# Attention followed by a gated MLP on one core: batch 0 in two K halves, weight blocks loaded in turn, a four-sum product form, a searched order

## The chip, the cores and the metric

The kernel runs on one core of one Trainium2 chip. The metric is the device time of one execution in microseconds (us), as a median of several executions. A profiled execution also gives a span, which is some 1.7 us shorter than the timed figure (259.1 against 260.84 us in the profiled run of the kernel before). For a program on one core a run is called slow when it lies over 1.5% above the fastest of its kernel; only fast runs enter the ratios below.

The program keeps its operands in SBUF and puts the products of TensorE in banks of PSUM (the pools with `space=PSUM`), from where VectorE and ScalarE read them. Engine names in the profile are PE (TensorE, the matrix products), PEld (its weight loads, which overlap: 193.8 us beside 241.7 us of PE in a span of 259.1 us in the kernel before), DVE (VectorE), ACT (ScalarE), POOL (GpSimd) and SP or SPq (SyncE, whose queue issues the DMAs).

## The reference

Eight batches, eight heads, 576 positions of 64 numbers each; 32 packed queries `p` per head. Attention packs the keys and values into 32 positions and lets `q` attend to those; a gated MLP follows.

```python
p_packed = sm_attn(p, k, v)                 # 8 x 8 x 32 x 64
out = sm_attn(q, p_packed, p_packed)        # 8 x 8 x 576 x 64, softmax(scale * q kT) v
x = out.transpose(0, 2, 1, 3).reshape(4608, 512)
h = x @ w_in                                # 512 -> 2048
g = h * (1.0 / (1.0 + np.exp(-beta * h)))
return g @ w_out                            # 2048 -> 512, float32
```

## The kernel before

The kernel never forms the attention output. It multiplies the packed values into `w_in` (products `w_ps`, scaled by beta into `W_bf`) and the softmax weights `A2T` into that (`h_ps`, the hidden layer). ScalarE turns `h_ps` into `g_main`. The second layer works on *units* of 256 positions: two for each batch, and two more (`g_rem`) that collect the 64 remaining positions of four batches each.

The instructions are not written in their order. Every piece of work is a task with an engine, an estimated duration, dependences and a rank, and a list scheduler, which runs when the kernel is built, emits them: each engine takes the ready task with the lowest rank. When TensorE has nothing ready before 48 us, it emits a small filler product (`warm_ps`), meant to keep its clock up: the granted clock of the profiled run is 1.00 from 0 to 210 us.

```python
WARM_UNTIL = 48.0
FIRST = "p k0 w_in0 k0r beta w_in2 v0 v0r q0 k1 k1r q0r v1 q1 v1r q1r w_out1 w_in1 w_in3 w_out2 w_out0 w_out3".split()
...
                if not can:
                    if e == "PE" and now < WARM_UNTIL:
                        self.filler()
                        free[e] = now + 0.11
                        moved = True
                    continue
                start(min(can, key=lambda t: t.rank))
```

`FIRST` ranks the first loads. The two units of batch 0 are *plain*: 16 products of 512 columns per half unit are summed in one PSUM bank over all of K, so they need all of `w_out`.

```python
            def product(i, x=x):                       # plan_plain
                ...
                for f in (2 * i, 2 * i + 1):
                    self.mm(st[*unit, "o", x][:], st[*unit, "g"][:, 2 * (f // 8) + x, f % 8, :], self.w_out_bf[:, f, :],
                            start=(f == 0), stop=(f == FT - 1))
            ...
            for i in range(8):
                last = self.task(("p", unit, x, i), "PE", 0.44, ...,
                    made + [("w_out", 2 * i), ("w_out", 2 * i + 1), last], ...)
```

The other 16 units are in *product form*: seven block products in place of eight (Strassen's kind), with sums of operands made on VectorE (`g_sums`, `w_mix`), products in four PSUM banks C, D, A, B, and five takes of 512 columns, four of them on VectorE, that combine the banks in SBUF (`o_sb`).

```python
            if i == 0:                                  # sums of a unit
                nc.vector.tensor_tensor(st[*unit, "S"][:, 0:2], g[:, 0:2], g[:, 2:4], ALU.add)
            elif i == 1:
                nc.vector.tensor_tensor(st[*unit, "S"][:, 2], g[:, 0], g[:, 3], ALU.add)
            else:
                nc.vector.tensor_tensor(g[:, 1:3], g[:, 1:3], g[:, 0:4:3], ALU.subtract)
```

The sums of the first softmax (`z1`) are ten products per batch against a matrix of ones, and their reciprocal is multiplied into the packed values. The last unit of all is a rest unit, stored by four DMAs.

The softmax here doesn't subtract the row's maximum and nothing guards it: scores larger than these inputs give would overflow.

## Time and profile before

| | before |
|---|---|
| time, median (lowest to highest) | 261.65 us (259.98 to 265.47), 3 runs |
| profiled span | 259.1 us |
| filler products of TensorE | 256, all before 50 us |
| VectorE / ScalarE busy | 199.2 us (77%) / 176.1 us (68%) |
| last product ends, span ends | 253.1 us, 259.1 us |

To read it: the busy share of TensorE (93%) counts filler as work. The useful split is between the start, where data is missing, and the rest, where TensorE is hardly ever idle.

### The profile page before, as it was taken

What the parts mean: (1) busy time and instruction counts of PE and PEld (TensorE: products, weight loads), DVE (VectorE), ACT (ScalarE), POOL (GpSimd) and SP (SyncE); (2) the same over time, 40 slices, a digit from 0 to 9 for tenths busy, and PEclk for the clock granted to TensorE, in tenths of its full rate; (3) what the DMA queues carried; (4) which work ended last, traced back from release to release, by engine and by line L of the source; (5) the groups of instructions that cost most, each with busy time, mean ns of one, the idle gap of its engine ahead of it and who ended that gap; (6) DMA issues with size and microseconds to landing.
All of it is one profiled execution on the core that took longest, in us unless ns stands there. A gap on an engine that the chain in (4) does not pass through costs nothing.

```text
span 259.1 us, 6793 instructions
## 1 busy us (share of the span) xinstructions
PE 241.7 (93%) x2897; PEld 193.8 (75%) x2897; DVE 199.2 (77%) x288; ACT 176.1 (68%) x308; POOL 63.4 (24%) x58
## 2 busy tenths in 40 slices
PE   4899689899989999998999999999999999999990
PEld 4897576566554878886778877877889778889880
DVE  6476766887985987796888968979996688665771
ACT  1153579867877878879786987886898768765000
POOL 4320433151440741342315231600900000000000
PEclk9999999999999999999999999999999999999999
DMA  7999999997998998996998999989660102201113
GB/s 225 352 320 268 280 325 384 348 330 183 288 199 237 292 246 235 212 333 148 265 251 263 143 318 291 205 227 272 174 172 7 79 0 83 82 27 60 81 81 81
DMA packets 73471, 54.18 MB, mean 209 GB/s; under 512 B 42065, under 2 KB 66657, under 8 KB 73441
## 3 DMA queue, kind: packets, MB, share of 16 engines
q1 hardware_dynamic: 73440, 53.76, 75.2%
q8 instruction: 22, 0.36, 0.6%
q14 instruction: 9, 0.07, 0.1%
HBM read 37.23 MB, written 9.44 MB: 180 GB/s over the span
## 4 chain that ended last, share of the span: by engine, by line
PE 56%; DMA 20%; SPq 10%; ACT 4%; issue 3%; POOL 3%; DVE 2%; POOLq 0%
PE o_ps L194 31%; PE h_ps L194 14%; DMA k<-in_k_dram 9%; SPq L336 5%; DMA v<-in_v_dram 4%; PE w_ps L194 3%; DMA qT<-q_bf 3%; SPq L250 2%; PE hr_ps L194 2%; DMA q32r<-in_q_dram 2%; DMA v32r<-in_v_dram 2%; PE z_ps L194 2%; PE s_ps L194 1%; SPq L242 1%; ACT g_main L639 1%
## 5 line engine op out<-in xcount | busy, mean ns | idle before, releaser
L639 ACT ACTIVATE g_main<-h_ps 128x512 bf16<-128x512 f32 x128 | 71.1, 596 | 29.5 <-PE h_ps L194 28.6
L194 PE MATMUL h_ps<-A2T,W_bf 128*128 128x256 bf16 x512 | 70.2, 273 | 0.6 <-ACT g_main L639 0.6
L194 PEld LDWEIGHTS <-W_bf 128*128 128x128 bf16 x768 | 57.1, 98 | 12.7 <-issue 4.7
L194 PE MATMUL o_ps<-w_mix,g_main 128*128 128x256 bf16 x448 | 59.5, 273 | 0.0
L194 PEld LDWEIGHTS <-g_main 128*128 128x128 bf16 x512 | 48.2, 98 | 12.5 <-issue 2.9
L600 DVE TENSOR_TENSOR W_bf<-w_ps,beta_bc 128x512 bf16<-128x512 f32 x64 | 41.5, 682 | 5.7 <-PE w_ps L194 5.2
L194 PEld LDWEIGHTS <-g_sums 128*128 128x128 bf16 x384 | 36.4, 98 | 5.5 <-issue 1.4
L209 ACT ACT_TABLE_LOAD x28 | 35.9, 1283 | 1.2 <-PEq L1067 0.7
L194 PE MATMUL o_ps<-w_out_bf,g_sums 128*128 128x256 bf16 x256 | 33.9, 273 | 0.0
L707 DVE TENSOR_TENSOR g_sums<-g_main 128x2048 bf16<-128x2048 bf16 x14 | 21.8, 1555 | 4.8 <-ACT g_main L639 4.8
L194 PE MATMUL warm_ps<-identr 128*128 128x128 bf16 x256 | 21.9, 237 | 3.7 <-DVE bones L858 3.7
L276 POOL CAST q_bf<-q 128x2048 bf16<-128x2048 f32 (+1 forms) x7 | 14.6, 2081 | 33.5 <-DMA q<-in_q_dram 19.9
L194 PEld LDWEIGHTS <-identr 128*128 128x128 bf16 x256 | 18.0, 108 | 5.5 <-DVE bones L858 3.7
L276 POOL CAST v_bf<-v 128x2048 bf16<-128x2048 f32 (+1 forms) x7 | 13.4, 1912 | 26.2 <-PE h_ps L194 9.8
L774 DVE TENSOR_TENSOR o_sb<-o_sb,o_ps 128x512 f32<-128x512 f32 x16 | 11.0, 685 | 10.0 <-ACT g_main L639 2.5
L541 DVE TENSOR_TENSOR A2T<-E2T,rz 128x512 bf16<-128x512 bf16 (+1 forms) x24 | 13.6, 587 | 5.5 <-ACT rz L536 5.5
L276 POOL CAST k_bf<-k 128x2048 bf16<-128x2048 f32 (+1 forms) x7 | 12.4, 1771 | 21.4 <-DMA k<-in_k_dram 10.4
L711 DVE TENSOR_TENSOR g_main<-g_main 128x2048 bf16<-128x2048 bf16 x14 | 17.4, 1244 | 0.0
L194 PE MATMUL o_ps<-w_mix,g_sums 128*128 128x256 bf16 x128 | 17.3, 273 | 0.0
L194 PE MATMUL o_ps<-w_out_bf,g_main 128*128 128x512 bf16 x64 | 17.0, 380 | 0.0
L772 ACT COPY o_sb<-o_ps 128x512 f32<-128x512 f32 x16 | 9.4, 588 | 10.3 <-PE o_ps L194 10.2
L194 PEld LDWEIGHTS <-pp 64*32 64x32 bf16 x384 | 6.0, 88 | 13.5 <-issue 10.9
(86 smaller groups left out, 296.5 us busy)
## 6 DMA issues: line engine op xcount, KB each, us to landing
out_dram<-o_sb SPq DMA_DIRECT2D x16, 512.0 KB, 3.9
k<-in_k_dram SPq DMA_DIRECT2D x7, 1024.0 KB, 8.5
v<-in_v_dram SPq DMA_DIRECT2D x7, 1024.0 KB, 6.8
q<-in_q_dram SPq DMA_DIRECT2D x7, 1024.0 KB, 6.7
w_in<-in_moe_w_in_dram SPq DMA_DIRECT2D x4, 1024.0 KB, 9.4
w_out<-in_moe_w_out_dram SPq DMA_DIRECT2D x4, 1024.0 KB, 12.4
k<-in_k_dram SPq DMA_DIRECT2D x2, 512.0 KB, 5.4
k32r<-in_k_dram SPq DMA_DIRECT2D x16, 64.0 KB, 5.2
```

The costliest lines, as they stand in the source:

```text
L194: return self.nc.tensor.matmul(out, lhsT, rhs, start=start, stop=stop, tile_position=pos, skip_group_check=True)
L209: self.nc.scalar.preload_act_table_set(SETS[mode])
L250: nc.sync.dma_start(t[64 * g : 64 * g + 64, :].rearrange("p (h d) -> p h d", h=4), src[b, 4 * g : 4 * g + 4, SM:S, :].rearrange("h p d -> ...
L276: self.copy[engine](self.t[b, x][:, 0:2048].rearrange("p (t h d) -> p h t d", t=4, h=8)[:, h], self.t[b, x, "32"][:].rearrange("p (h t d) ...
L336: nc.sync.dma_start_transpose(t[:], st[b, x][:])
L541: nc.vector.tensor_tensor(part(st[b, "A2"], i), part(st[b, "E2"], i), part(st[b, "rz2"], i), ALU.mult)
L600: nc.vector.tensor_tensor(st[b, "W"][:, r, cols], st[b, "w", m][:], self.beta_bc[:, cols], ALU.mult)
L639: nc.scalar.activation(st[b, v, "g"][:, :, f, :], st[b, "h", v, f][:].rearrange("p (q n) -> p q n", q=4), AF.Silu)
L707: nc.vector.tensor_tensor(st[*unit, "S"][:, 0:2], g[:, 0:2], g[:, 2:4], ALU.add)
L711: nc.vector.tensor_tensor(g[:, 1:3], g[:, 1:3], g[:, 0:4:3], ALU.subtract)
L772: nc.scalar.copy(middle, st[*unit, "C"][:])
L774: nc.vector.tensor_tensor(ends, middle.rearrange("p (h n) -> p h n", h=2)[:, ::-1], halves(st[*unit, "D"]), ALU.subtract)
```

## The change

The intent is to start real work of TensorE earlier. Units of batch 0 are multiplied in two halves over K (the first half needs only `w_in` blocks 0 and 2 and `w_out` blocks 0 and 2), and the halves are added in SBUF; the loads of `w_in` and `w_out` are listed in turn. The first loads of `q` get buffers of their own. Along with it come a product form with four sums of 128x1024 and seven takes of 256 columns, a cheaper normalisation, four output buffers instead of two, and a last unit that is no rest unit, so that its store is one DMA. A table of 1,135 rank offsets, given by the number of the task, replaces the earlier tuning of the order.

```diff
+OUTS = 4
-FIRST = "p k0 w_in0 k0r beta w_in2 v0 v0r q0 k1 k1r q0r v1 q1 v1r q1r w_out1 w_in1 w_in3 w_out2 w_out0 w_out3".split()
+FIRST = "p beta k0 k0r v0 v0r w_in0 q0 q0r w_in2 w_out0 w_out2 k1 k1r v1 v1r q1 q1r w_in1 w_in3 w_out1 w_out3".split()
+OFFSETS = {0: -15, 1: -1.5, 2: -13.6, 3: -197.8, 4: -84.8, 5: -114.5, 6: -25.9, 7: -74.5, 10: -239.3, 11: 106.1, ...
     # (many lines of numbers cut)
     def add(self, engine, us, fn, deps=(), rank=0, ...):
+        rank += OFFSETS.get(len(self.tasks), 0)
 ...
     # plan_plain: two K halves
+        for s in range(2):
+            order = [(8 * kh + f, 8 * kh + f + 1) for f in range(4 * s, 4 * s + 4, 2) for kh in range(2)]
+            for x in range(2):
 ...
-                    made + [("w_out", 2 * i), ("w_out", 2 * i + 1), last], ...
+                        [made[f % 8] for f in order[i]] + [("w_out", f) for f in order[i]] + [last], ...
 ...
+                    if s == 0:
+                        nc.scalar.copy(o, ps)
+                    else:
+                        nc.vector.tensor_tensor(o, o, ps, ALU.add)
 ...
     # plan_unit: four sums, seven takes
+                0: (s[:, 0], a21, a22, ALU.add),
+                1: (s[:, 1], s[:, 0], a11, ALU.subtract),
+                2: (s[:, 2], a12, s[:, 1], ALU.subtract),
+                3: (a21, a11, a21, ALU.subtract),
 ...
+        takes = [(0, 1, False), (0, 0, True), (3, 1, False), (1, 0, False), (1, 1, True), (3, 0, True), (2, 0, False)]
 ...
+            if added:
+                nc.vector.tensor_tensor(o, o, ps, ALU.add)
             else:
+                self.copy[engine](o, ps)
 ...
     # sums of the first softmax: columns of one number
-                        ps[64 * r : 64 * r + 64, 0:128].rearrange("p (c j) -> p c j", c=NC),
-                        self.ones64[:],
-                        E()[:, t, :].rearrange("p (c r j) -> p r c j", c=NC, r=2)[:, r],
+                        ps[:, r : r + 1],
+                        E()[:, t, 128 * r : 128 * r + 128],
+                        self.eights[:],
 ...
+            nc.scalar.activation(st[b, "E2"][:, i, 0:SM], st[b, "s2", i][:], AF.Exp, scale=st[b, "rz1"][:, i : i + 1])
 ...
     # casts on GpSimd in pieces of two heads
+                m = 2 if engine == "POOL" else n
+                for j in range(0, n, m):
+                    self.copy[engine](to[:, j : j + m], of[:, j : j + m])
```

## The prediction

> **What bounds the kernel now.** I read first the busy table and the 40 slices of the page, then sums over windows, then TensorE's own timeline, and last the chain that ended last.
>
> ```profile
> PE 241.7 (93%) x2897; PEld 193.8 (75%) x2897; DVE 199.2 (77%) x288; ACT 176.1 (68%) x308; POOL 63.4 (24%) x58
> PE   4899689899989999998999999999999999999990
> ACT  1153579867877878879786987886898768765000
> DMA  7999999997998998996998999989660102201113
> ```
>
> TensorE is the busiest engine, but its 93% hides filler: in the first eight slices (52 us) ACT is mostly idle, so little real work can be flowing. DMA is full up to about 190 us. The windows and groups say how much of TensorE's time is filler:
>
> ```profile
> 30.00:40.00 10.00, 8.56 (x150) 7.21 (x148) 6.97 (x15) 8.37 (x18) 3.35 (x4) 1.00 1.08 336
> ...
> 90.00:110.00 20.00, 20.00 (x228) 15.87 (x227) 16.17 (x25) 16.36 (x30) 7.01 (x6) 1.00 0.94 230
> ...
> 190.00:210.00 20.00, 20.00 (x258) 16.56 (x256) 15.43 (x25) 15.97 (x27) 0.00 (x0) 1.00 0.20 67
> ```
>
> ```profile
> L194 PE MATMUL warm_ps<-identr 128*128 128x128 bf16 x256 | 21.9, 237 | 3.7 <-DVE bones L858 3.7
> ```
>
> (Columns of a window: length, then busy and count of PE, PEld, DVE, ACT, POOL; granted clock, DMA share, GB/s.) In the two late windows TensorE has no gap at all, and all 256 filler products (warm_ps) lie before 50 us. So there are two stages. Up to 50 us TensorE waits for data while it is kept warm; from 50 us to the last product at 253.2 us it is saturated: its idle time over 50 to 210 us is 0.42 + 0.79 + 0.96 = 2.2 us.
>
> How much real work there is, I get from start-to-start distances in TensorE's timeline, not from the mean durations (273 ns for a 256-column product, which overlap):
>
> ```profile
> 93.84 1.04 PE L194 MATMUL h_ps<-A2T,W_bf 128*128 128x256 bf16 x8
> 94.80 0.41 PE L194 MATMUL w_ps<-w_in_bf,pp 64*32 64x512 bf16 x8
> ```
>
> ```profile
> 237.83 15.30 PE o_ps L194 x140
> ```
>
> The last line is from the chain: 140 products in 15.3 us, 0.109 us each. Eight w_ps cost about 0.43 us with the change of tiling before them. The sum: hidden layer 512 x 0.109 = 55.9; its rests 256 x 0.03 = 7.6; second layer in product form 896 x 0.109 = 97.8; plain form 64 x 0.216 = 13.8; w_ps 32 x 0.43 = 13.8; attention (s1, z1, packed, s2, z2) about 22; transposes, beta and p about 9. Together some 220 us. From 50 to 253.2 us some 201 of them run, before 50 us only about 19 to 20. So about 30 us of the first 50 are lost, 2.5 us later, and 6 us in the tail (253.2 to 259.1: the last addition and the last store). A gain must come from the 30 us, as no term of the 220 shrinks much.
>
> Why they are lost is in the order of loads. The rate there is about 313 GB/s and what batches 0 and 1 and both weights need is 16 MB (p 0.5, six loads of 1.18, weights 8.4), which is 51 us. Before, all weights of the second layer come late:
>
> ```profile
> 31.23 0.60 SPq L965 DMA_DIRECT2D w_out<-in_moe_w_out_dram  x1
> 31.87 1.80 SPq L965 DMA_DIRECT2D w_in<-in_moe_w_in_dram  x2
> 34.21 3.66 SPq L965 DMA_DIRECT2D w_out<-in_moe_w_out_dram  x2
> ```
>
> and its first product starts at 52.3 us; before 50 us there are 39 of the 512 h_ps products and no o_ps.
>
> [...] So splitting a plain product in two K halves costs TensorE nothing, since number and width of the matmuls stay.
> [...]
> [...] the 128x2048 sum takes 1214 ns without casts beside it (the two rest units) and 1555 ns on average where casts run.
> [...]
>
> **The change, part by part.**
>
> *Batch 0 in two halves, loads in turn.* The new order is p, k0, v0, w_in0, q0, w_in2, w_out0, w_out2, then k1, v1, q1, then the other four weight blocks. Adding up bytes with the DMA rates of the slices before (225, 352, 320, 268, 280, 325, 384 GB/s per 6.48 us), I estimate v0 landed at 10.5 us, q0 at 17, w_in2 at 21, w_out0 at 25, w_out2 at 28, q1 at 40, w_in1 and w_in3 at 42 and 45, w_out3 at 51 to 54. The packed keys no longer wait for the 0.95 us reciprocal. Then A2 of batch 0 is ready near 25 us (31.4 to 34.4 before), and two blocks of work become possible: half of h of batch 0, 8 tasks x 8 x 0.109 = 7.0 us, and the first K half of its plain products, 32 x 0.216 = 6.9 us. Before, only 4.3 us of h had run by 50 us. Against a perfect packing I get 28 us of real work by 44 us and no loss from there on (the other half of h of batch 0 and the first half of h of batch 1 are ready): a loss of 16 to 20 us in place of 30, so a gain of 10 to 14. I choose 11, since the casts of w_out (16 x 0.48 us on VectorE) and the single table switch lie in the way. On VectorE the halves cost four more takes, split with ScalarE; off the path.
>
> *Four-sum form.* TensorE still has 56 products of 256 columns per unit, so 0. VectorE: sums before 1.555 + 1.131 + 1.244 = 3.9 us per unit; after, four 128x1024 sums at 0.68 (undisturbed) to 1.0, 2.7 to 4. Takes before 4 x 0.685 = 2.7; after 6 x 0.42 = 2.5. Some 1 us per unit, 16 us in all over 16 units, but VectorE is at 80% behind a saturated TensorE: off the path, near 0. The new risk is on TensorE: seven products go through two PSUM banks, and product i waits for the take of product i - 2. One product is 8 x 0.109 = 0.87 us and a take is 0.42 plus two hand-overs, about 0.8: it just fits if VectorE is free, and costs up to 0.7 us if a sum or a W_bf runs then. There are 5 such places in 16 units, 80; most have hidden-layer products between. I put +1.5 us.
>
> *Normalisation.* The 8 reciprocals fall from 0.95 us to about 0.16, W_bf becomes a three-input form at some 0.74 in place of 0.68 (64 x 0.06 = +3.8 us of VectorE), the exps get +0.09 x 32 = 3 us of ScalarE, z1 saves TensorE 0.1 x 8 = 0.8 us. Path: -0.8.
>
> *Weight sums* four at 1.26 us in place of five: off the path. *Four output buffers and later stores:* stores wait for nothing now that bounds TensorE: 0. *Tail:* the last store is now one DMA and not four with 0.6 us of issue each, and the last take has 256 columns: -0.5.
>
> *Supply of batch 2.* At 84.75 us, where h of batch 2 starts, two units of batch 1 (100 products, 10.9 us) are left in stock. If 11 us more are done early, that stock is gone then, and DMA, full until 190 us, must bring batch 2 earlier. q0 and q1 get buffers of their own, so k2 and v2 need not wait; I expect h of batch 2 some 4 to 6 us sooner. I put +1 us of idle.
>
> Sum: -11 + 1.5 - 0.8 - 0.5 + 1 = -9.8 us; from 261.65 that is 251.9. I take 251.5.
>
> **Rivals.** First, DMA stays the bound: the 16 MB still land at about 51 us, and each batch after takes DMA some 23 us (transposes of q start at 71.0, 92.5, 116.2, 141.2, 164.4, 187.2 us) against 25 of TensorE. For it: the chain gives DMA 20%, and TensorE twice waits near 0.8 to 1 us for the transposed q. Against it: after 190 us TensorE works 63 us without loads, so the stock only grows. Then early work turns into idle time at batch 2 or 3: 255 to 259.
> Second, the PSUM hand-over of the four-sum form bites: 80 places x 0.15 us = 12 us, which eats the gain: 258 to 264. Against it: VectorE gets emptier, and products of other batches can lie between.
> Third, the pieces fit better than I trust: dense work from 25 us on, h of batch 2 by 76 us: 245 to 248.
>
> **Range and chances.** The size of the early gain (8 to 15 us) and the two losses (0 to 6) give 245.5 to 257.5. Two per cent is 5.2 us, so faster needs a net gain of over 5.2: the early part alone gives twice that, and both rivals together would have to take half of it. Faster 0.81, same 0.16, slower 0.03.
>
> **What would show it.** Right: o_ps products before 40 us; A2T of batch 0 near 25 us; about 30 us of real TensorE work before 50 us and fewer warm_ps; TensorE full from 45 us; the last product 9 to 10 us sooner; VectorE busy 10 to 25 us less. Wrong: gaps of TensorE behind o_sb takes on VectorE (second rival); gaps near 75 to 85 us that end with qT (first rival); first o_ps product later than 45 us because w_out's casts come late.

## More of the kernel before

One more line of the page, the chain of work that ended last as shares by engine, will matter for the comparison:

```profile
PE 56%; DMA 20%; SPq 10%; ACT 4%; issue 3%; POOL 3%; DVE 2%; POOLq 0%
```

Only 56% of the chain that sets the end is TensorE; 30% is transfers (loads, and transposes done by DMA) and their issue.

## The result

| | before | changed |
|---|---|---|
| time, median (lowest to highest), 4 runs each | 261.4 us (259.98 to 265.47) | 252.35 us (251.76 to 252.49) |
| ratio of fast runs | | 0.9645, 95% interval 0.958 to 0.971 |
| profiled span | 259.1 us | 250.0 us |

The changed kernel is faster, and the predicted 251.5 us is 0.85 us from the median. One of the four runs before, 265.47 us, is slow by the rule above. Ratios here are from the fast runs of a kernel and of the kernel before in the same rounds, so they are not quite the ratios of the medians quoted (the means of the fast runs of this table give 0.967, inside the interval).

The views of the changed kernel follow in the order of the prediction. First the page's busy times and slices (each digit tenths of a 6.25 us slice):

```profile
PE 237.0 (95%) x2852; PEld 191.1 (76%) x2852; DVE 174.1 (70%) x327; ACT 176.6 (71%) x312; POOL 71.0 (28%) x119
...
PE   4999879899999999999999999999999999999993
...
ACT  2276357697879896898889867987699868875200
...
DMA  6999999999999999999999699999937020111042
```

TensorE is busy for 4.7 us less and VectorE for 25.1 us less, and ScalarE for as long as before. DMA is still full until about 181 us (29 slices).

The same windows as before (length, then busy time and count of PE, PEld, DVE, ACT, POOL; granted clock, DMA share, GB/s), and the group of the filler:

```profile
30.00:40.00 10.00, 8.11 (x122) 6.25 (x121) 7.39 (x15) 5.41 (x11) 3.61 (x7) 1.00 1.07 337
...
90.00:110.00 20.00, 20.00 (x255) 15.99 (x254) 15.51 (x31) 16.55 (x31) 6.53 (x13) 1.00 1.06 266
190.00:210.00 20.00, 20.00 (x264) 16.62 (x262) 13.77 (x26) 15.74 (x28) 0.00 (x0) 1.00 0.17 61
```

```profile
L294 PE MATMUL warm_ps<-identr 128*128 128x128 bf16 x211 | 18.3, 239 | 3.7 <-DVE bones L980 3.7
```

The late windows are saturated as before. There are only 45 filler products fewer, and the window from 30 to 40 us is no fuller. The start improved less than it looks from the total. TensorE's timeline shows what starts when:

```profile
31.93 1.04 PE L294 MATMUL h_ps<-A2T,W_bf 128*128 128x256 bf16 x8
...
40.91 1.03 PE L294 MATMUL o_ps<-w_out_bf,g_main 128*128 128x512 bf16 x4
```

The hidden layer begins at 31.93 us, 1.8 us earlier than before (33.72 us). The second layer begins at 40.91 us, 11 us earlier (before 52.3 us). VectorE's timeline and the DMA queue's say why `h_ps` did not come sooner (a bracket holds the idle time before an instruction and what ended it):

```profile
23.69 0.69 DVE L651 TENSOR_TENSOR A2T<-E2T,z_ps 128x512 bf16<-128x512 bf16 x1
24.79 0.69 DVE L651 TENSOR_TENSOR A2T<-E2T,z_ps 128x512 bf16<-128x512 bf16 x1 [0.41 <-ACT z_ps L646]
...
28.38 0.69 DVE L1106 CAST w_in_bf<-w_in 128x1024 bf16<-128x1024 f32 x1 [1.30 <-DMA w_in<-in_moe_w_in_dram]
28.99 1.40 DVE L709 SCALAR_TENSOR_TENSOR W_bf<-w_ps,rz,beta_bc 128x512 bf16<-128x512 f32 x2
...
35.04 0.49 DVE L1120 TENSOR_SCALAR w_out_bf<-w_out,rbeta 128x512 bf16<-128x512 f32 x1 [1.67 <-DMA w_out<-in_moe_w_out_dram]
```

```profile
18.77 1.16 SPq L1089 DMA_DIRECT2D w_in<-in_moe_w_in_dram  x2
...
25.43 0.63 SPq L1089 DMA_DIRECT2D w_out<-in_moe_w_out_dram  x1
...
32.27 1.57 SPq L1089 DMA_DIRECT2D w_out<-in_moe_w_out_dram  x1
33.95 2.75 SPq L1089 DMA_DIRECT2D w_in<-in_moe_w_in_dram  x2
```

The two main blocks of the softmax weights `A2T` are there by 25.5 us (33.6 us before), but `W_bf` then waits for `w_in`, which is issued only at 18.77 us. The queue does not follow the listed order: k1 goes out at 14.40 us, ahead of the first `w_in`, because the rank offsets apply to loads as well. The first `w_out` block lands at 35.02 us and the second at 41.96 us.

The chain of work that ended last, as shares by engine, and two of its pieces:

```profile
PE 82%; DMA 9%; DVE 3%; SPq 2%; POOL 1%; issue 1%; ACT 0%; POOLq 0%; DVEq 0%
```

```profile
33.95 10.71 DMA w_in<-in_moe_w_in_dram
...
232.73 13.11 PE o_ps L294 x120
```

TensorE now holds 82% of the chain in place of 56%. What is left of loads there is the start: of the last two blocks of `w_in`, issued from 33.95 us on, one lands at 44.66 us (the other at 47.38), and the chain goes over it. After 50 us the list of TensorE's waits (us in total, times, longest) is nearly empty, and none of them is a take of `o_ps`:

```profile
PE w_ps L294 <- DVE pp L584: 0.3, 1, 0.3
PE h_ps L294 <- ACT g_rem L770: 0.2, 1, 0.2
PE h_ps L294 <- ACT g_main L748: 0.2, 1, 0.2
```

The ends of both timelines, first before, then changed:

```profile
253.15 0.69 DVE L782 TENSOR_TENSOR o_sb<-o_sb,o_ps 128x512 f32<-128x512 f32 x1 [0.19 <-PE o_ps L194]
253.87 2.46 SPq L809 DMA_DIRECT2D out_dram<-o_sb  x4
```

```profile
245.87 0.42 DVE L882 COPY o_sb<-o_ps 128x256 f32<-128x256 f32 x1 [0.45 <-PE o_ps L294]
246.32 0.34 SPq L916 DMA_DIRECT2D out_dram<-o_sb  x1
```

The last take is 0.27 us shorter and the issue of the last store 2.1 us shorter.

To add these up, I went through TensorE's whole timeline with start-to-start distances, took out the idle time in brackets, and counted filler apart. "Lost" is filler plus idle.

| us of the profiled run | before | changed | gain |
|---|---|---|---|
| lost before 50 us (filler + idle) | 18.91 + 9.16 = 28.07 | 16.90 + 7.47 = 24.37 | 3.70 |
| idle after 50 us | 2.15 | 0.74 | 1.41 |
| real work, whole run | 222.89 | 220.73 | 2.16 |
| of it before 50 us (50 less what is lost) | 21.9 | 25.6 | 3.7 more |
| last product to end of span | 5.95 | 4.12 | 1.83 |
| span | 259.1 | 250.0 | 9.1 |

The four gains (3.70, 1.41, 2.16 and 1.83) sum to 9.10 us, the gain in span. The expectation of e4 below counts the last row 0.2 us longer on both sides (6.15 and 4.32), with the same difference.

### The profile page after: what moved, and what is told of

Its sections match the earlier page's. It is cut to its first block, busy times and chain, and to the rows that moved or that the text cites.

```text
span 250.0 us, 6818 instructions
## 1 busy us (share of the span) xinstructions
PE 237.0 (95%) x2852; PEld 191.1 (76%) x2852; DVE 174.1 (70%) x327; ACT 176.6 (71%) x312; POOL 71.0 (28%) x119
## 4 chain that ended last, share of the span: by engine, by line
PE 82%; DMA 9%; DVE 3%; SPq 2%; POOL 1%; issue 1%; ACT 0%; POOLq 0%; DVEq 0%
PE o_ps L294 44%; PE h_ps L294 22%; DMA v<-in_v_dram 5%; DMA w_in<-in_moe_w_in_dram 4%; PE w_ps L294 4%; PE hr_ps L294 3%; PE warm_ps L294 2%; PE s_ps L294 2%; PE z_ps L294 2%; SPq L364 1%; PE pp_ps L294 1%; DVE identr L976 1%; POOL w_in_bf L1104 1%; DVE pT L1026 1%; DVE k_bf L394 0%
## 5 line engine op out<-in xcount | busy, mean ns | idle before, releaser
L709 DVE SCALAR_TENSOR_TENSOR W_bf<-w_ps,rz,beta_bc 128x512 bf16<-128x512 f32 x64 | 44.8, 745 | 7.4 <-PE w_ps L294 7.2
L294 PE MATMUL o_ps<-w_out_bf,g_main 128*128 128x256 bf16 (+1 forms) x288 | 46.6, 296 | 0.7 <-DVE w_out_bf L1120 0.7
L882 DVE COPY o_sb<-o_ps 128x256 f32<-128x256 f32 x48 | 20.2, 422 | 28.1 <-PE o_ps L294 27.5
L294 PE MATMUL o_ps<-w_mix,g_sums 128*128 128x256 bf16 x256 | 34.6, 273 | 0.0
L394 POOL CAST v_bf<-v 128x512 bf16<-128x512 f32 x26 | 18.1, 736 | 47.7 <-PE o_ps L294 22.5
L294 PE MATMUL o_ps<-w_mix,g_main 128*128 128x256 bf16 x224 | 31.4, 273 | 0.0
L880 DVE TENSOR_TENSOR o_sb<-o_sb,o_ps 128x256 f32<-128x256 f32 x48 | 20.1, 419 | 13.5 <-PE o_ps L294 13.0
L394 POOL CAST q_bf<-q 128x512 bf16<-128x512 f32 x26 | 16.7, 684 | 18.6 <-DMA q<-in_q_dram 13.1
L394 POOL CAST k_bf<-k 128x512 bf16<-128x512 f32 x26 | 15.4, 634 | 14.0 <-DMA k<-in_k_dram 4.1
L294 PE MATMUL o_ps<-w_out_bf,g_sums 128*128 128x256 bf16 x128 | 17.3, 273 | 0.0
```

Source lines behind the costliest of these rows:

```text
L294: return self.nc.tensor.matmul(out, lhsT, rhs, start=start, stop=stop, tile_position=pos, skip_group_check=True)
L394: self.copy[engine](to[:, j : j + m], of[:, j : j + m])
L709: nc.vector.scalar_tensor_tensor(st[b, "W"][:, r, cols], st[b, "w", m][:], st[b, "rz1"][:, r : r + 1], self.beta_bc[:, cols], ALU.mult, AL ...
L880: nc.vector.tensor_tensor(o, o, ps, ALU.add)
L882: self.copy[engine](o, ps)
```

## The experiments

My theory after the result: the gain comes from the start, through the early halves, and from the tail; the four-sum form is off the path. Rivals: the searched order (the offsets) alone does it; or the new form does; or the hand-over of PSUM banks already costs something. Twelve kernels were run in three calls. The median of the kernel before was 261.51, 262.65 and 263.15 us in the three, so kernels of different calls are compared by their ratios.

| kernel | median us | ratio to before [95%] |
|---|---|---|
| changed | 252.35 | 0.9645 [0.958, 0.971] |
| e1 no offsets | 265.49 | 1.0169 [1.0108, 1.0231] |
| e2 halves late | 269.17 | 1.0304 [1.0248, 1.0359] |
| e4 last store in four | 253.21 | 0.9701 [0.9658, 0.9743] |
| e7 listed order of first loads | 299.94 | 1.1502 [1.1431, 1.1573] |
| s1 before, order searched | 269.93 | 1.0164 [1.0077, 1.0250] |
| s2 halves late, order searched again | 261.72 | 0.9955 [0.9884, 1.0026] |
| s3 changed, order searched from nothing | 257.82 | 0.9810 [0.9758, 0.9862] |
| s4 old form in the changed kernel, searched | 257.97 | 0.9820 [0.9745, 0.9894] |
| e8 takes doubled | 259.34 | 0.9862 [0.9827, 0.9896] |
| e9 no offsets, filler until 60 us | 262.73 | 1.0036 [1.0010, 1.0063] |
| e10 last store in halves | 252.27 | 0.9611 [0.9562, 0.9661] |
| s6 searched further | 254.12 | 0.9663 [0.9612, 0.9714] |

All gave correct results.

### First call: one part undone at a time

**e1_no_offsets** leaves the structure and drops the searched offsets.

```diff
-        rank += OFFSETS.get(len(self.tasks), 0)
```

> The changed kernel with the table of per-task rank offsets emptied; every task, size and buffer stays. If the gain of 9 us is in the structure (halves, form, tail), this should stay within 253 to 256 us. If it is in the searched order, it should fall back to 259 to 263 us, with TensorE idle time after 50 us well above the 0.7 us of the changed kernel.

Measured: 265.49 us, 1.7% slower than the kernel before. The structure without its order gains nothing. TensorE's timeline shows the loss, and the windows show a second effect:

```profile
54.67 0.22 PE L293 MATMUL z2r_ps<-E2T,bones 128*128 128x128 bf16 x1 [2.18 <-ACT E2T L620]
...
59.09 1.89 PE L293 MATMUL h_ps<-A2T,W_bf 128*128 128x256 bf16 x8
```

```profile
55.00:56.00 1.00, 0.58 (x8) 0.11 (x7) 1.00 (x4) 0.95 (x4) 0.00 (x0) 1.00 1.05 341
56.00:57.00 1.00, 0.74 (x8) 0.20 (x7) 1.00 (x3) 0.86 (x1) 0.00 (x0) 0.61 1.15 223
57.00:58.00 1.00, 0.96 (x8) 0.10 (x2) 1.00 (x3) 0.00 (x0) 0.00 (x0) 0.50 1.12 246
```

After a wait of 2.18 us, and a few short ones, with no filler left to emit after 48 us, the granted clock falls to 0.50 until 63 us, and eight `h_ps` products take 1.89 us in place of 1.04. The clock is at 0.50 twice: from 35.73 to 39.15 us (3.42 us; the mean clock from 35 to 40 us is 0.66) and from 56.21 to 63.04 us (6.83 us). So this run mixes two causes, and e9 below parts them.

**e2_late_halves** keeps two halves but gives the first half the first eight blocks of K and lets every product wait for all of `g_main` and of `w_out`, as before the change.

```diff
-            order = [(8 * kh + f, 8 * kh + f + 1) for f in range(4 * s, 4 * s + 4, 2) for kh in range(2)]
+            order = [(8 * s + f, 8 * s + f + 1) for f in range(0, 8, 2)]
...
-                        [made[f % 8] for f in order[i]] + [("w_out", f) for f in order[i]] + [last],
+                        made + [("w_out", f) for f in range(FT)] + [last],
```

> The changed kernel with batch 0's plain products made to wait for all of the hidden units and all of w_out, in plain K order; same tasks, same takes. If the early half products are what fills the first 50 us (23 products of 0.216 us = 5.0 us before 50 us), this costs 4 to 5 us: 256 to 258 us, no o_ps product before about 53 us. If the start is gained in the loads and the attention alone, 252 to 253 us.

Measured: 269.17 us. Real work before 50 us falls from 25.6 to 20.9 us, but idle time after 50 us rises from 0.74 to 6.5 us and the clock falls to half speed from 49.5 to 56.4 us and from 134.9 to 138.3 us (mean clock 0.84 from 50 to 70 us, 0.91 from 130 to 150 us), so the run does not say how much is due to the halves: the offsets were searched for another set of dependences. Inconclusive in size; s2 repeats it with the order searched again.

**e4_store_in_four** issues the last store as four DMAs.

```diff
+            if unit == (B - 1, 1):
+                for e in range(4):
+                    h = slice(64 * (e % 2), 64 * (e % 2) + 64)
+                    dma(rows[h, 2 * v + e // 2, :], o[h, e // 2, :])
```

> The changed kernel with its very last store sent as four DMAs instead of one. The tail (last product to end) went from 6.15 to 4.32 us; if that is the issue time of three more DMAs on SyncE (0.6 us each), this costs 1.4 to 1.8 us: 253.8 to 254.2 us. If the shorter tail comes from the smaller last take and the transfer itself, 252.2 to 252.7 us.

Measured: 253.21 us, 0.86 us over the median of the changed kernel. The intervals of the two ratios overlap, so the reading rests on the two traces: from the last product to the end it is 4.84 us in place of 4.12. The tail of the timeline shows four issues that overlap the last take:

```profile
246.72 2.39 SPq L919 DMA_DIRECT2D out_dram<-o_sb  x4
247.15 0.42 DVE L882 COPY o_sb<-o_ps 128x256 f32<-128x256 f32 x1 [0.45 <-PE o_ps L294]
```

Each issue takes about 0.6 us on the queue (2.39 / 4). Here, though, the first issues start before the last take, since their columns are ready; that is probably why three more issues cost 0.7 us of tail and not 1.8. So the single store explains about 0.7 of the 1.8 us that the tail gained. The take of 256 columns in place of 512 gives 0.27. The rest (about 0.8) I did not isolate; in the kernel before nothing could be issued ahead of the last addition, because that addition wrote columns of every part.

**e7_first_order** keeps the offsets except on the first loads, which then follow `FIRST` as the prediction assumed.

```diff
-        rank += OFFSETS.get(len(self.tasks), 0)
+        if not (engine == "SP" and rank < -900):
+            rank += OFFSETS.get(len(self.tasks), 0)
```

> The changed kernel with no offsets on the first loads only, so that they are issued in the listed order (v0, w_in0, q0, w_in2, w_out0, w_out2, then batch 1), which my prediction took for granted; the trace shows another order (q0 first, batch 1's keys before w_in). If the listed order lets h and the half products start near 25 to 30 us, 248 to 251 us. If the other offsets only fit the order that was searched with them, 253 to 258 us.

Measured: 299.94 us, the largest effect of all. TensorE's longest waits:

```profile
PE w_ps L295 <- DVE A2T L652: 9.3, 3, 6.2
PE h_ps L295 <- ACT g_main L749: 7.9, 13, 3.9
```

TensorE is idle for some 32 us after 50 us, and the mean granted clock is below 1.00 in six of the 12 stretches of its table of windows (lowest 0.75, from 210 to 230 us). It does not mean that the listed order of loads is bad in itself (e1 and e9 load in that order too): the other ranks were searched together with the loads, and they do not fit any other set. It does mean that an offset table is one object, and that reading `FIRST` alone tells little of the order that runs.

### Second call: the order searched again for each structure

To compare structures fairly I searched orders myself. The kernel's list scheduler predicts an end from its own durations, and a random search (annealing) on that predicted end tried 2.2 to 2.4 million changes of offsets for each kernel. s2 started from the changed kernel's offsets; the other three started without any. Only the offsets differ, apart from the part named.

**s1_before_searched**: the kernel before, with a line that adds offsets found by this search.

```diff
+        rank += OFFSETS.get(len(self.tasks), 0)
```

> The kernel before, unchanged but for a table of per-task rank offsets found by 2.4 million trials of its own scheduler (which then puts its end 0.4 us sooner). If ordering alone could have given the gain, 252 to 256 us; if the old structure has nothing left for the order to find, 260 to 262 us, with as many filler products (about 250) as before.

Measured: 269.93 us (two of its four runs were slow; the two fast ones are 265.87 and 268.23), so slower than the hand-tuned order. The scheduler had predicted 258.8 us. TensorE waits 2.7 us for a transposed q and 2.2 us for a transposed k, waits for DMAs, to which the scheduler gives fixed durations. A better order for the old structure may exist; this search did not find one, so the rival "order alone" is not supported, though not excluded.

**s2_late_searched**: the edit of e2, and offsets searched again.

> The changed kernel with late half products (they wait for all hidden units and all of w_out), with the order searched again for that, 2.3 million trials from the changed kernel's own order. If the early halves are worth what TensorE does before 50 us (4 to 5 us), 255.5 to 257.5 us, far below the 269.2 us of the run without a new search, whose excess was the order. If the halves are worth nothing once the order fits, 252 to 253.5 us. If late halves cost what the first run said, 265 us or more.

Measured: 261.72 us, the same as before within the interval. Against the changed kernel that is 0.9955 to 0.9645, 3.1%, or 8 us. Lost before 50 us: 19.7 + 10.3 = 30.0 us, worse than the kernel before, with 20.0 us of real work there. Idle time after 50 us is 2.95 us. In the profiled run the clock was at half speed from 21.7 to 25.1 us and, after a wait of 3.25 us for the cast of k, from 31.9 to 35.4 us (mean clock 0.69 from 30 to 35 us; s3 has one such stretch, from 28.7 to 32.1 us, with 0.79 from 30 to 35 us). That is not the main cause: another of s2's runs took 262.92 us with a mean clock of 0.999.

**s3_new_form_searched** and **s4_old_form_searched**: s3 is the changed kernel with its offsets thrown away and searched from nothing, as a control of the search; s4 is the same with the old sums, products, takes and weight sums put back.

```diff
-MIX = ('DVE', 'DVE', 'DVE', 'DVE')
+MIX = {3: 'DVE', 4: 'DVE', 7: 'DVE', 6: 'DVE', 1: 'DVE'}
 # plan_unit, operands, products and takes as in the kernel before
```

> The changed kernel, its offsets emptied and searched again from nothing with 2.2 million trials (a shallower search than the one it came with). Control for the next run. Its scheduler puts it at 258.1 us; by the runs so far the chip should show 257 to 260.5 us.

> The changed kernel with the old five-sum product form in place of the four-sum form (banks C, D, A, B, five takes of 512 columns, five weight sums), everything else kept, searched with as many trials as the control. If the form is off the path, as I predicted, within 1 us of the control; if the four sums and the shorter holds of PSUM banks matter, 1.5 to 4 us slower than the control, with VectorE about 15 us busier.

Measured: 257.82 and 257.97 us, intervals almost the same. VectorE is busy for 178.5 us with the new form and 185.9 with the old. So, with orders searched equally, the form makes no difference of more than about 1%, which is what the intervals leave; nothing speaks for its being on the path. The control also measures the search: mine ends 1.65% above the order that came with the change. That matters for s2: against s3 the early halves are worth 0.9955 to 0.981, 1.5% (3.8 us); against the changed kernel 3.1% (8 us). The first comparison sets two of my searches against each other, the second one of mine against the better order; this is as narrow as the runs make it, and the intervals of s2 and s3, though apart, leave nearly 1% either way on top.

### Third call: the slack of the takes, the clock, the store

**e8_takes_doubled** puts a copy of the same PSUM block into a spare tile in front of each of the 96 VectorE takes.

```diff
+            if added or engine == "DVE":
+                nc.vector.tensor_copy(self.spare[:], ps)
```

> The changed kernel with one more VectorE instruction ahead of each of VectorE's 96 takes (it reads the same PSUM columns into an unused tile, 0.42 us), the order untouched. It lengthens every hand-over of the four-sum form by 0.42 us, from about 0.8 to 1.2 us against 0.87 us of the product between. If the hand-over just fits (my prediction charged 1.5 us for it), TensorE now waits up to 0.35 us at many of the 80 places: 15 us or more of idle time, 262 us or more. If other products lie between nearly everywhere, 253 to 257 us, with the idle time gathered in the last 15 us.

Measured: 259.34 us, 7.0 us more than the changed kernel's median; the last product ends 8.0 us later. VectorE is 30.4 us busier. TensorE's waits that were not there before:

```profile
PE o_ps L294 <- DVE o_sb L884: 1.2, 3, 0.7
PE o_ps L294 <- DVE o_sb L882: 1.0, 3, 0.6
```

That is 2.2 us of the 8; the rest is spread over gaps too short for the trace to name (idle time after 50 us rises by 2.3 us in all, and start-to-start distances of real products by 5.9, of which 3.4 stand at the 256-column `o_ps` products: 114.9 ns apart on average in place of 111.1). Sums and `W_bf` on VectorE stand on its chain as well, so this run tells that slack is short, not which of them uses it up. 96 added copies of 0.419 us are 40.2 us (30.4 of busy time, as neighbours overlap), and they cost 8: most of it is still absorbed, but the slack is short of one take's length in places.

**e9_no_offsets_warm** is e1 with filler until 60 us.

```diff
-WARM_UNTIL = 48.0
+WARM_UNTIL = 60.0
-        rank += OFFSETS.get(len(self.tasks), 0)
```

> The run without offsets (265.5 us), with filler products allowed until 60 us instead of 48, so that TensorE isn't left idle at 52 to 57 us, where that run's clock fell (0.83 granted in 50 to 70 us, eight h products in 1.89 us). If the fallen clock was part of its loss, 261.5 to 263.5 us with a granted clock of 1.0 throughout; if not, 265 to 266 us.

Measured: 262.73 us, ratio 1.0036 against 1.0169 for e1, with the granted clock at 1.00 in every window to 230 us. So 1.3% (3.5 us) of e1's loss was the fallen clock. The other 3.9% (1.0036 to 0.9645, 10 us) is the order itself. With no searched order at all, the new structure only equals the tuned kernel before.

This run also tells where the order pays. Its loads go out as `FIRST` lists them, and `w_out` blocks 0 and 2 land at 27.3 and 30.1 us, far sooner than in the changed kernel; but q0 lands only at 21.4 us and `A2T` is there at 30.2 us. TensorE's timeline:

```profile
31.81 0.49 PE L293 MATMUL h_ps<-A2T,W_bf 128*128 128x256 bf16 x3
...
38.12 0.38 PE L293 MATMUL o_ps<-w_out_bf,g_main 128*128 128x512 bf16 x1
```

The hidden layer begins as with the searched order (31.93 us there), and 25.9 us of real work are done by 50 us (25.6 there). The difference comes later: filler and idle time after 50 us are 5.2 + 3.4 = 8.6 us in place of 0.74.

**e10_store_in_halves** stores the last unit in two DMAs, so that the first can leave before the last take.

```diff
+            self.task(("store", unit), "SP", 0.9, lambda: half(1), deps, -10)
+            self.task(None, "SP", 0.9, lambda: half(0), [deps[j] for j in (0, 1, 3, 4)], -10)
```

> The changed kernel with the last unit's store in two halves, the first sent as soon as its two quarters are done (two takes, about 1.7 us, before the last). If the transfer's size matters in the tail of 4.3 us, 0.4 to 0.9 us less: 251.4 to 252 us. If the tail is a fixed time from issue to landing, no change, or 0.3 us more for the second issue.

Measured: 252.27 us, ratio 0.9611 [0.9562, 0.9661] against 0.9645 [0.958, 0.971] of the changed kernel. The intervals overlap widely. Inconclusive; if there is a gain, it is a few tenths of a per cent.

**s6_search_tail** takes the halves of e10 and searches the order further from the changed kernel's own, in an attempt to beat it.

> The changed kernel with its order searched further (its own scheduler gains 0.7 us on it) and the last store in halves: an attempt at a version that beats both. 250.5 to 252 us if both carry over to the chip; 252 to 255 us if the last tenths of the order are fitted to the scheduler's durations and not to the chip's.

Measured: 254.12 us (one of six runs slow). The scheduler predicted 1.55 us less than for the changed kernel (251.92 against 253.47), and the chip gave nothing of it: the profiled run has 2.45 us of idle time after 50 us in place of 0.74. At this level the search fits the model's durations, not the chip's. No version here clearly beats the changed kernel.

Not undone singly in any run: the buffers of q, the four output buffers, the normalisation and the casts in pieces.

## Why the prediction was right

The total was right, the range held, and the mechanism was right in outline: TensorE stays saturated in between, and the start and the tail, which were to give all of the gain but 0.8 us, give 5.5 of the 9.1 us. The terms were less good than their sum.

| term | predicted | measured |
|---|---|---|
| early work | -11 | -3.7 in time lost before 50 us |
| bank hand-over and supply of batch 2 | +1.5 and +1 | -1.4 in idle time after 50 us |
| real work (z1) | -0.8 | -2.2 |
| tail | -0.5 | -1.8 |
| sum | -9.8 | -9.1 |

**The early term was oversized.** Two steps of it failed. The first is "half of h of batch 0, 8 tasks x 8 x 0.109 = 7.0 us". A task is four products, not eight: the 512 `h_ps` products are 64 for each batch, so the half is 32 products or 3.5 us, and just these 32 run before 50 us (39 before the change). That is 3.5 of the 7.3 us by which the term was too large. The second is "Adding up bytes with the DMA rates of the slices before". Even where the loads do go out in the assumed order (e9), v0, q0, `w_in` 2, `w_out` 0 and `w_out` 2 land at 13.2, 21.4, 24.7, 27.3 and 30.1 us, where 10.5, 17, 21, 25 and 28 were forecast. In the changed kernel the offsets reorder the first loads as well. "A2 of batch 0 is ready near 25 us" came true (25.5 us), but by an order that loads q0 first of all and `w_in` and `w_out` late (`w_out` 0 and 2 land at 35.0 and 42.0 us); in the assumed order it is 30.2 us. With either order the hidden layer begins at 31.8 to 31.9 us. The "28 us of real work by 44 us" became 25.6 us by 50. What was gained are 23 plain products of the second layer, 23 x 0.216 = 5.0 us, less 7 products of the hidden layer (0.8 us), which is about the rise of real work there (3.7 us). How the other 3.8 us of the miss divide between late landings and imperfect packing stays open.

**The halves are the means.** s2 shows it: without early halves, and with an order searched for that case, the time returns to that of the kernel before. In size the runs leave 1.5 to 3.1%, before noise.

**The losses that were set against it did not come.** The supply of batch 2 was to cost 1 us: its hidden layer starts at 84.89 us against 84.75, so not sooner by 4 to 6 us, and TensorE is full there all the same. My reading is that with only 3.7 us more done early the stock of batch 1 was not used up, so this rival had no chance to act. The hand-over was to cost 1.5: the list of waits after 50 us has no `o_ps` in it. The list leaves out waits under 0.15 us, but nothing hides there: the 256-column `o_ps` products start 111.1 ns apart on average, 111.6 before. Under the doubled takes of e8 the list has them. Of the "about 0.8" us that the prediction put for a take and two hand-overs, the take is 0.42 as assumed. One hand-over can be read: in 20 cases in which VectorE stood idle before, its take began 0.31 us after the start of the last `o_ps` product. The way back to TensorE was not measured singly, so the 0.8 stays an estimate. Of the idle time that went, 1.7 us were waits for transposed q before; the list of the changed kernel has none of them.

**Real work and tail were undersized.** z1 gives 1.0 us by start-to-start distances (0.8 predicted; its ten products of one column start 25 ns apart, 0.25 us in all). The remaining 1.2 us is spread over many groups; some matmul records are missing in each trace, so I do not read a cause into it. Splitting the plain products into halves cost TensorE nothing, as predicted: in both kernels they are 64 products of 512 columns, 216 ns apart (median). The tail counted only part of three saved issues; it gave 1.8 us, of which e4 explains about 0.7.

**Off the path, as predicted.** VectorE fell by 25.1 us (the upper end of the "10 to 25" predicted), with takes of 422 and 419 ns where the prediction put 0.42 us, and sums of 687 to 719 ns on average (780 to 832 in the two rest units). The reciprocals fell from 954 to 160 ns and `W_bf` rose from 682 to 744, as predicted; the four weight sums took 1412 ns on average, where 1260 was predicted from the five before. s3 and s4 show no gain in time from it. Some 10 of the 25 us are not the form but the time by which sums beside GpSimd's casts ran longer than undisturbed ones (1216 ns for 128x2048, 685 for 128x1024): 11.4 us over all 48 sums before, 1.8 us over the 64 after. The prediction read the mean of 1555 ns as the time of a sum beside casts; it is a mixture, since ten of the 14 sums took 1208 to 1224 ns and four, beside casts, 1796 to 2914. ScalarE's busy time did not change, but the exps did get longer: 684 ns in place of 594, 90 ns each, where the prediction put 0.09 us; other work on ScalarE got shorter (the copies of `o_sb`, 8.2 in place of 9.4 us).

**The rivals.** The first, supply, is right about the start alone: the chain of the changed kernel still runs over one of the last `w_in` blocks, which lands at 44.66 us. It is wrong about later batches. The second did not act, and e8 shows how near it is. The third would have needed dense work from 25 us.

**What the prediction did not see.** It treated the offsets as incidental. Without them the same structure is 5.2% slower (e1: 1.0169 against 0.9645), a quarter of it by the clock. The prediction's reason for its 11 us was a perfect packing, and an order of that quality is exactly what a search had to supply. Structure and order gain together or not at all in these runs; that the errors of the terms cancelled in the sum (7.3 too much for early work, 3.9 too much for losses, 1.4 and 1.3 too little for real work and tail) is luck. Two readings of the start were off as well, with little effect: 21.9 us of real work run before 50 us, not 19 to 20, and ScalarE is busy for about half of the first eight slices, not "mostly idle".

## What to carry to other kernels

Split the matrix engine's time into real work, filler and idle by stage before valuing a change: a share of 93% hid 19 us of filler at the start. Work that needs only part of the weights fills such a start, but only as far as all its inputs are there: with those weights sooner and q later (e9) the hidden layer began no earlier, so read the landings of all of them from the trace rather than from a list in the source. When a static schedule was searched, any change of structure needs a new search before it is judged, and a search on modelled durations stops paying once its gains are as small as its model's errors; keep filler available for as long as waits can occur (e9 against e1: 1.0036 in place of 1.0169). Before two blocks of work are added up, count their products in the trace.

## What else these traces show

- The clock. Stretches at half speed lasted 3.4 to 3.5 us (e1 from 35.73 us, s2 from 21.7 and from 31.9, s3 from 28.7, e2 from 134.9) or about twice that (6.83 us in e1, 6.9 in e2). In the 3.41 us ahead of a fall TensorE's timeline names 2.02 and 2.45 us of idle time in e1, in two pieces each, 1.51 and 3.25 us in s2, 2.37 in s3 and 2.94 in e2 (at 49.5 us). The amount alone does not settle it: between 50.57 and 53.03 us s3 has 1.87 us of idle time, and its clock is 1.00 from 50 to 60 us. So these runs show no threshold.
- A sum beside a cast. Before, with GpSimd's casts in one piece of 128x2048, a 128x1024 sum in bf16 took up to 2374 ns (684 undisturbed) and a 128x2048 sum up to 2914 (1215); in the changed kernel, with casts in pieces of 128x512, a 128x1024 sum took at most 1102.
- The issue of a store holds the queue of SyncE for 0.34 us for one of 512 KB at the end of the changed kernel, and for 0.6 us for each of four of 128 KB (2.39 us in e4).
- Orders searched for a static schedule: the same structure took 252.35, 257.82, 265.49 and 299.94 us here with four orders.
